# Turning q and k of five more blocks by transposing DMA instead of TensorE, in a sliding-window attention with an MLP behind it

## The chip, the cores and the metric

The kernel runs on one core of one Trainium2 chip. The metric is the device time of one launch in microseconds, as the median of the runs.

## What is computed

Eight batches, eight heads, 576 positions, 64 numbers a head. Attention with an ALiBi bias looks back over at most 128 positions; the heads are laid side by side to rows of 512, which go through a layer norm, an MLP of width 2048 with ReLU, and a residual.

```python
scores = scale * np.matmul(q, k.transpose(0, 1, 3, 2))
rel = pos[:, None] - pos[None, :]
bias = slopes[:, None, None] * (-np.abs(rel).astype(np.float32))[None, :, :]
mask = (rel >= 0) & (rel < window)          # window = 128
scores = np.where(mask, scores + bias[None], -1000000000.0)
attn = softmax(scores)
x = np.matmul(attn, v)                      # then (B, S, H * D)
xn = (x - mu) / np.sqrt(var + 1e-06) * g_ln
out = x + np.maximum(xn @ w_ch1, 0.0) @ w_ch2
```

(The softmax is written out in the reference.) Inputs and outputs are fp32; the kernel loads q, k, v and the weights as fp16, and sums in fp32.

## The kernel before

**Tiles.** The batches go in four pairs p = 0 to 3. A pair has four row blocks i of 128 positions, each for both batches, and a tail i = 4 of 64 positions of each batch together. So a pair has nine blocks of 128 rows, blk = 2i + b for i < 4 and blk = 8 for the tail; n = 9p + blk numbers all 36 (`order`). The third pair is p = 2, its blocks are n = 18 to 26, and its last five are blk 4 to 8, that is i = 2, 3 and 4.

**Loads.** GpSimd issues the loads with a cast to fp16 (`load_qk`, `load_v`), in the order of the list `loads`. The step of block n asks for all loads up to block n + 6 (`load_until`). The raw q and the raw k of a turn each take one of 4 buffers (`raw_pool`), so the load of turn t = 5p + i reuses the buffer of turn t - 4 and waits until that one has been read.

**Turns.** The scores need q and k with the head dimension on partitions. `turn(p, i)` makes that, in one of two ways:

- By TensorE (pairs 0 to 2 before): 64 transposes of 64x64 (32 for a tail) by `transposed()` (L301) into PSUM, with two copies on DVE and two on ACT to SBUF (L333, L334; for a tail one on each, L338). With `in_sc` the PSUM used is that of the score banks, which are marked as `junk`; the next scores in a marked bank are computed whole by `seen()` (L395), otherwise only the parts that the window can see.
- By DMA (pair 3 before): four `dma_start_transpose` of 128x512 on SP (two for a tail, L322), from raw tiles that were loaded in another layout: q in four DMAs of 64 KB and k in two of 128 KB, where the other way has two of 128 KB each; a tail has two and two of 64 KB in both.

`by_dma` tells which way a turn goes.

**Scores and values.** `scores` (L436 the matmuls, L445 the exponential on ACT, L456 the decay mask on DVE), then `values` (L489 on TensorE, L497 and L498 on DVE) give the rows x. `stats` takes mean and variance on DVE (L586, L587) and 1/sqrt on GpSimd (L541, L544); `normal` makes the normed row on DVE (L528) and turns it by a transposing DMA on SP (L536) into xT.

**MLP.** Blocks are gathered in twelve groups: six of two, then six of four; groups 6 to 11 hold blocks 12 to 15, 16 to 19, 20 to 23 and so on. `mlp1` (L730) and `mlp2` (L763) run the two products; from group 6 on `fast_mlp2` (L829) does the second in seven half-size products with sums of `ht` on DVE (L798) and of the results on DVE (L847), over a ring of four PSUM banks. Results are stored by SP (L925; L921 for a tail).

**Order.** TensorE, SP, ACT and DVE run in the order in which the program writes them (`manual_schedule`); GpSimd's order is the scheduler's. `steps` lists the attention work, and `weave_at` puts its steps between units of the MLP (a unit is one `ht` tile of `mlp1`, or one product or part of one in the second half). From block 8 on, an iteration n adds four steps: the values of block n with the scores of block n + 2; masks and stats of n; `turn_at(n + 1)`; `normal(n)`. For a group of four, `mlp1` takes steps at units 0, 2, 5, 7, 8, 10, 13, 15 and `fast_mlp2` at 1, 3, 6, 7, 7, 10, 12, 13. `turn_at` puts a turn by TensorE four iterations ahead of its block and a turn by DMA five:

```python
ahead = [m for m in (n + 3, n + 4) if m < count and order[m][1] % 2 == 0]
return [f for m in ahead if by_dma(order[m][0]) == (m == n + 4) for f in turn_step(m, True)]
```

So the turns of (p, i) = (2, 2), (2, 3) and (2, 4), for blocks 22, 24 and 26, stand in the iterations 18, 20 and 22, and that of (3, 0), for block 27, also in iteration 22.

Of the kernel before, what the change touches and what calls it, by code (L numbers as in the profile page):

```python
# [26 lines left out]
FAST = 6  # L27

NV = 10
BY_DMA_TURN = 3  # L30
AHEAD = 6

FIRST_GROUPS, FIRST = 2, 4
# [26 lines left out]
def kernel(  # L60
# [146 lines left out]

    raw = {}

    def by_dma(p):  # L210
        return p >= BY_DMA_TURN

    def load_qk(src, tag, p, i):

        n = min(P, S - i * P)
        t = raw_pool.tile([P, H, 2, D], FP16, tag=tag, name=tag)
        raw[tag, p, i] = t
        if by_dma(p):
            t = raw[tag, p, i] = t.rearrange("p h r d -> p (h r d)").rearrange(
                "p (b h d) -> p b h d", b=2, h=H  # L220
            )
            for b in range(2):
                rows = src[2 * p + b, :, i * P : i * P + n, :]
                if i == 4:
                    parts = [(t[b * n : (b + 1) * n, 0], rows)]
                elif tag == "k":
                    parts = [(t[:, b], rows)]
                else:
                    rows = rows.rearrange("h (c r) d -> h r c d", r=2)
                    parts = [  # L230
                        (t[r * HALF : (r + 1) * HALF, b], rows[:, r]) for r in range(2)
                    ]
                for dst, part in parts:
                    nc.gpsimd.dma_start(out=dst, in_=part.rearrange("h p d -> p h d"))
            return
        for b in range(2):
            nc.gpsimd.dma_start(  # L237
                out=t[b * n // 2 : (b + 1) * n // 2],
                in_=src[2 * p + b, :, i * P : i * P + n, :].rearrange(
                    "h (c r) d -> c h r d", r=2  # L240
                ),
            )
# [10 lines left out]
    order = [(p, blk) for p in range(NPAIR) for blk in range(NSLOT)]  # L253
# [3 lines left out]
    for n, (p, blk) in enumerate(order):  # L257
        if blk % 2 == 0:
            for src, tag in ((q, "q"), (k, "k")):
                loads.append((load_qk, src, tag, p, blk // 2))  # L260
        loads.append((load_v, p, blk))
        place.append(len(loads))
        loads += weights.get(n, [])
# [14 lines left out]
    def warm(n):  # L278

        if n:  # L280
            ps = ps_mm.tile([P, 4 * P], FP32, tag="mm", name="ps_warm")
        for _ in range(n):
            nc.tensor.matmul(ps, ones[:, 0:P], ones, start=True, stop=True)  # L283
# [7 lines left out]
    def transposed(tag, p, i, ps):  # L291


        st = raw.pop((tag, p, i))
        for hp in range(HP):
            for r in range(2):
                for b, dst in enumerate(ps):
                    rows = slice(b * HALF, (b + 1) * HALF)
                    for j in range(2):
                        cols = slice(j * HALF, (j + 1) * HALF)  # L300
                        nc.tensor.transpose(  # L301
                            dst[cols, r, hp, :],
                            st[rows, 2 * hp + j, r, :],
                            iden[rows, rows],
                        )

    def turn(p, i, in_sc=False, copies=(nc.vector.tensor_copy, nc.scalar.copy)):

        k = keys_tile("k", p, i)
        q = queries(p, i) if i < 4 else keys_tile("q", p, i)
        if by_dma(p):
            for tag, dst in (("q", q), ("k", k)):
                src = raw.pop((tag, p, i))
                for b in range(2 if i < 4 else 1):
                    t = dst[:, b]
                    if tag == "q" and i < 4:  # L320
                        t = turned["q", p, i][:, b].rearrange("p h r c -> p h (r c)")
                    nc.sync.dma_start_transpose(  # L322
                        out=t, in_=src[:, b].rearrange("p h d -> p (h d)")
                    )
            return
        ps = [bank(b if in_sc else None) for b in range(2)]
        if i < 4:
            transposed("q", p, i, [t[:, 0] for t in ps])
            if p == 0 and i == 1:
                warm(3)  # L330
            transposed("k", p, i, [t[:, 1] for t in ps])
            for b, copy in enumerate(copies):
                copy(out=q[:, b], in_=ps[b][:, 0])  # L333
                copy(out=k[:, b].rearrange("p h (c r) -> p r h c", r=2), in_=ps[b][:, 1])  # L334
        else:
            for tag, t, dst, copy in zip("qk", ps, (q, k), copies):
                transposed(tag, p, i, [t[:, 0]])
                copy(out=dst[:, 0].rearrange("p h (c r) -> p r h c", r=2), in_=t[:, 0])  # L338

    def bank(sc=None):  # L340
        if sc is None:
            return ps_mm.tile([P, 2, 2, HP, HALF], FP16, tag="mm", name="ps_tr")
        junk[sc] = True
        return ps_sc[sc][:, 0].bitcast(FP16).rearrange(
            "p (t r h c) -> p t r h c", t=2, r=2, h=HP
        )

    def queries(p, i):
        if by_dma(p):
            t = turned_pool.tile([P, 2, HP, 2, HALF], FP16, tag="q", name="q")  # L350
            turned["q", p, i] = t
            return t
        t = turned_pool.tile([P, 2, 2, HP, HALF], FP16, tag="q", name="q")
        turned["q", p, i] = t.rearrange("p b r h c -> p b h r c")
        return t

    def keys_tile(tag, p, i):
        t = turned_pool.tile([P, 2, HP, P], FP16, tag=tag, name=tag)
        turned[tag, p, i] = t
        return t  # L360

    def turn_first():

        q, k = queries(0, 0), keys_tile("k", 0, 0)
        ps = [bank(b)[:, 0] for b in range(2)]
        transposed("q", 0, 0, ps)
        for b in range(2):
            nc.vector.tensor_copy(out=q[:, b], in_=ps[b])
        ps_row = spread_g()
        warm(2)  # L370
        ps = [bank(b)[:, 0] for b in (0, None)]
        transposed("k", 0, 0, ps)
        for b, copy in enumerate((nc.scalar.copy, nc.vector.tensor_copy)):
            copy(out=k[:, b].rearrange("p h (c r) -> p r h c", r=2), in_=ps[b])
        nc.vector.tensor_copy(out=g_row, in_=ps_row)
# [244 lines left out]
    for g, size in enumerate(GROUPS):  # L620
        n = sum(GROUPS[:g])
# [5 lines left out]
    def turn_step(n, *how):  # L627
        p, blk = order[n]
        return [(turn, p, blk // 2) + how]
# [54 lines left out]
    def turn_at(n):  # L684
        ahead = [m for m in (n + 3, n + 4) if m < count and order[m][1] % 2 == 0]
        return [
            f
            for m in ahead
            if by_dma(order[m][0]) == (m == n + 4)
            for f in turn_step(m, True)  # L690
        ]

    steps.append(turn_at(8))
    for n in range(8, count):
        first_half, second_half = values_steps(n)
        step = first_half + second_half[:1]
        if n + 1 < count and order[n + 1][1] == T:
            step += [(scores_tail, order[n][0])]
        if n + 2 < count:
            step += scores_step(n + 2)  # L700
        steps.append(step)
        steps.append(
            [m for t in (n + 1, n + 2) if t < count for m in masks_of(t)] + [(stats, n)]
        )
        if n + 1 < count:
            steps.append(turn_at(n + 1))
        steps.append([(normal, n)])
# [293 lines left out]
```

## Time and profile before

| | |
|---|---|
| runs of the kernel | median 319.14 us (318.6 to 319.21, three runs) |
| the profiled execution | 318.21 us, span 316.4 us |
| TensorE, matmuls | 305.0 us (96%), granted clock 0.996 of full |
| DVE / ACT / GpSimd | 228.1 us (72%) / 179.3 (57%) / 124.9 (39%) |
| L301, transposes of q and k on TensorE | last at 178.3 us, 864 weight loads |
| L322, transposing DMAs of q and k on SP | 18, from 173.7 us on |
| loads of q and k, GpSimd | L237 60 (pairs 0 to 2), L234 28 (pair 3) |

The chain of waits is followed back from the last instruction: each piece waited for the one before it, so its rows tell what set the end, with start, length, engine, tile, line and count. A timeline has the instructions of one engine in order, and in brackets the idle time before one with what ended it; on SP and GpSimd its times are those in which the engine issues a DMA, and the landing of the data comes later. Seen over 40 slices, TensorE is full from the middle on:

```profile
PE   8989999999898999999999999999999999999994
PEld 2468655857657667555885588548855875685483
DVE  2679787877667698768995889479948995761363
```

By group, TensorE's time goes to the MLP above all:

```profile
L730 PE MATMUL ps_r<-xT,w1g 128*128 128x512 f16 x384 | 85.1, 379 | 0.0
L763 PE MATMUL ps_m<-w,ht 128*128 128x512 f16 x192 | 46.0, 380 | 1.2 <-ACT ht L746 1.2
L829 PE MATMUL ps_r<-w,ht 128*128 128x256 f16 x384 | 44.1, 273 | 0.0
```

The last columns are the busy time of the group, the mean of one in ns, and the idle time of the engine before them with what ended it.

### The profile page before, as it was taken

The numbers are of one execution on the slowest core, as the hardware profiler recorded it, in microseconds if no ns is written. First come the engines' busy times: TensorE is split into PE (matmuls) and PEld (weight loads), VectorE is DVE, ScalarE is ACT, GpSimd is POOL, SyncE is SP. The second block draws the span as 40 slices with busy tenths as digits, with TensorE's granted clock in tenths as the row PEclk, the third lists the DMA queues.
The fourth block names the chain that finished last, engine by engine and source line by source line (L and its number), as shares of the span: only waits on it lengthen the run. The fifth ranks groups of instructions, "written<-read, shape, count | busy, mean of one in ns | idle before, by whom it ended". The sixth has DMA issues, their size and how long they took to land.

```text
span 316.4 us, 9932 instructions
## 1 busy us (share of the span) xinstructions
PE 305.0 (96%) x4195; PEld 205.2 (65%) x4195; DVE 228.1 (72%) x547; ACT 179.3 (57%) x311; POOL 124.9 (39%) x196
## 2 busy tenths in 40 slices
PE   8989999999898999999999999999999999999994
PEld 2468655857657667555885588548855875685483
DVE  2679787877667698768995889479948995761363
ACT  6488765667556658368347832772487247405600
POOL 8923758767155356484345572240001001100000
PEclk9999999999999999999999999999999999999998
DMA  9999999999996999499949994992348044015005
GB/s 111 164 206 199 190 145 184 200 140 149 86 118 79 107 99 157 52 144 68 76 52 158 171 124 53 143 158 52 83 89 132 15 87 86 19 26 125 0 0 136
DMA packets 121183, 34.68 MB, mean 110 GB/s; under 512 B 112049, under 2 KB 116785, under 8 KB 121138
## 3 DMA queue, kind: packets, MB, share of 16 engines
q0 software_dynamic: 89216, 18.36, 71.2%
q1 hardware_dynamic: 31442, 15.15, 25.6%
q8 instruction: 33, 0.54, 0.7%
q10 hardware_dynamic: 480, 0.52, 0.6%
q14 instruction: 12, 0.10, 0.1%
HBM read 36.90 MB, written 9.44 MB: 146 GB/s over the span
## 4 chain that ended last, share of the span: by engine, by line
PE 86%; DVE 6%; ACT 4%; issue 1%; POOL 1%; DVEq 0%; ACTq 0%; POOLq 0%
PE ps_r L730 27%; PE ps_r L829 23%; PE ps_m L763 11%; PE ps_m L730 10%; PE ps_sc L436 5%; PE ps_sc L301 3%; PE ps_r L489 3%; PE ps_pv L489 2%; PE ps_warm L283 2%; ACT probs L445 2%; DVE o L906 1%; DVE x L498 1%; DVE probs L456 1%; DVE o L847 1%; PE ps_tx L581 1%
## 5 line engine op out<-in xcount | busy, mean ns | idle before, releaser
L730 PEld LDWEIGHTS <-w1g 128*128 128x128 f16 x640 | 60.4, 98 | 50.6 <-DVE x L498 1.8
L730 PE MATMUL ps_r<-xT,w1g 128*128 128x512 f16 x384 | 85.1, 379 | 0.0
L445 ACT ACTIVATE probs<-ps_sc 128x1024 f16<-128x1024 f32 x56 | 54.2, 1026 | 51.6 <-PE ps_sc L436 51.5
L746 ACT ACTIVATE ht<-ps_r 128x512 f16<-128x512 f32 x96 | 56.2, 600 | 31.6 <-PE ps_r L730 31.5
L541 POOL TENSOR_TENSOR rstd<-moments,powers 128x1 f32<-128x1 f32 x28 | 6.8, 243 | 102.5 <-DVE moments L587 102.5
L763 PE MATMUL ps_m<-w,ht 128*128 128x512 f16 x192 | 46.0, 380 | 1.2 <-ACT ht L746 1.2
L829 PE MATMUL ps_r<-w,ht 128*128 128x256 f16 x384 | 44.1, 273 | 0.0
L247 POOL DMA_DIRECT2D vx<-in_v_dram x40 | 34.7, 883 | 22.1 <-PE ps_r L489 9.0
L456 DVE TENSOR_TENSOR probs<-probs,m 128x1024 f16<-128x1024 f16 x56 | 37.4, 688 | 7.4 <-ACT probs L445 7.2
L829 PEld LDWEIGHTS <-ht 128*128 128x128 f16 x384 | 37.1, 98 | 4.8
L746 ACT ACTIVATE ht<-ps_m 128x256 f16<-128x256 f32 x91 | 32.9, 391 | 8.5 <-PE ps_m L730 6.2
L730 PE MATMUL ps_m<-xT,w1g 128*128 128x256 f16 x256 | 31.5, 273 | 2.2 <-DVE x L498 0.8
L763 PEld LDWEIGHTS <-ht 128*128 128x128 f16 x192 | 17.1, 98 | 18.8 <-issue 1.3
L237 POOL DMA_DIRECT2D q<-in_q_dram x30 | 20.5, 690 | 17.3 <-PE ps_sc L301 9.3
L586 DVE BATCH_NORM_STATS2 st<-x 128x6 f32<-128x512 f16 x36 | 24.6, 684 | 0.0
L237 POOL DMA_DIRECT2D k<-in_k_dram x30 | 20.2, 687 | 5.8 <-DMA w<-in_moe_w_ch_dram 4.2
L436 PE MATMUL ps_sc<-q,k 64*64 64x128 f16 (+1 forms) x1088 | 20.4, 209 | 1.6 <-ACT probs L445 1.1
L829 PE MATMUL ps_r<-w,hs 128*128 128x256 f16 x192 | 21.9, 273 | 0.0
L489 PEld LDWEIGHTS <-probs 128*128 128x128 f16 x448 | 18.8, 97 | 4.7 <-DVE probs L456 0.3
L829 PEld LDWEIGHTS <-hs 128*128 128x128 f16 x192 | 18.8, 98 | 2.2
L847 DVE TENSOR_TENSOR o<-ps_r,o 128x512 f32<-128x512 f32 (+1 forms) x25 | 16.1, 655 | 5.0 <-PE ps_r L829 4.9
L528 DVE TENSOR_SCALAR xc<-x,moments,rstd 128x512 f16<-128x512 f16 x28 | 12.0, 430 | 10.3 <-POOL rstd L544 10.3
(87 smaller groups left out, 384.3 us busy)
## 6 DMA issues: line engine op xcount, KB each, us to landing
out_dram<-o SPq DMA_DIRECT2D x66, 128.0 KB, 3.1
k<-in_k_dram POOLq DMA_DIRECT2D x32, 128.0 KB, 6.2
vx<-in_v_dram POOLq DMA_DIRECT2D x32, 128.0 KB, 6.7
w<-in_moe_w_ch_dram POOLq DMA_DIRECT2D x8, 512.0 KB, 11.3
q<-in_q_dram POOLq DMA_DIRECT2D x24, 128.0 KB, 4.3
q<-in_q_dram POOLq DMA_DIRECT2D x24, 64.0 KB, 3.8
k<-in_k_dram POOLq DMA_DIRECT2D x8, 64.0 KB, 4.6
vx<-in_v_dram POOLq DMA_DIRECT2D x8, 64.0 KB, 6.4
```

The source lines that it names most:

```text
L237: nc.gpsimd.dma_start(out=t[b * n // 2 : (b + 1) * n // 2], in_=src[2 * p + b, :, i * P : i * P + n, :].rearrange("h (c r) d -> c h r d", ...
L247: nc.gpsimd.dma_start(out=vx[p0 : p0 + n, :, 0:D], in_=v[b, :, t0 : t0 + n, :].rearrange("h p d -> p h d"),)
L436: nc.tensor.matmul(in_halves(ps[cols, j, n, t, :])[:, r, queries], kt[rows, hp, cols], in_halves(qt[rows, b, hp])[:, r, queries], start=Tr ...
L445: nc.scalar.activation(out=dst.rearrange("p (n j) q -> p j n q", j=2), in_=ps.rearrange("p j n t q -> p j n (t q)"), func=AF.Exp, scale=in ...
L456: nc.vector.tensor_tensor(out=dst, in0=dst, in1=mask, op=ALU.mult)
L489: nc.tensor.matmul(ps[:, i, :], pr[:, h, t, :], vext[(p * NSLOT + o) % NV][:, h, :], start=(n == 0), stop=(n == len(terms) - 1),)
L586: nc.vector.bn_stats(out=st, in_=xs[order[n]])
L730: nc.tensor.matmul(ps[:, 0:cols], w[:, kb, fb * P : (fb + 1) * P], xT[:, kb, 0:cols], start=(kb == 0), stop=(kb == NKB - 1),)
L746: nc.scalar.activation(out=ht[:, fb, 0:cols], in_=ps[:, 0:cols], func=AF.Relu)
L763: nc.tensor.matmul(sums[at], ht[:, fb, at * P : (at + 1) * P], w2[:, fb, :], start=(fb == 0), stop=(fb == NFB - 1),)
L829: nc.tensor.matmul(banks[name][pair][:, pair, :], lhs[:, fb, pair * P : (pair + 1) * P], rhs[:, fb, :], start=(first and fb == 0 and (pair ...
L847: nc.vector.tensor_tensor(out=o[:, at, cols], in0=banks[name][at.start][:, at, :], in1=(x if to_x else o)[:, at, cols], op=ALU.add,)
```

## The change

`BY_DMA_TURN` becomes a pair and row block, (2, 2) in place of 3, and `by_dma` takes both. The turns (2, 2), (2, 3) and (2, 4) then go the way of pair 3: loads in the other layout, a contiguous q tile, ten transposing DMAs on SP, and a place one iteration earlier in `turn_at`. The last turn by TensorE is (2, 1).

```diff
-BY_DMA_TURN = 3
+BY_DMA_TURN = (2, 2)
...
-    def by_dma(p):
-        return p >= BY_DMA_TURN
+    def by_dma(p, i):
+        return (p, i) >= BY_DMA_TURN
...
-        if by_dma(p):
+        if by_dma(p, i):
             t = raw[tag, p, i] = t.rearrange("p h r d -> p (h r d)").rearrange(
...
-        if by_dma(p):
+        if by_dma(p, i):
             for tag, dst in (("q", q), ("k", k)):
...
     def queries(p, i):
-        if by_dma(p):
+        if by_dma(p, i):
             t = turned_pool.tile([P, 2, HP, 2, HALF], FP16, tag="q", name="q")
...
-            if by_dma(order[m][0]) == (m == n + 4)
+            if by_dma(order[m][0], order[m][1] // 2) == (m == n + 4)
             for f in turn_step(m, True)
```

## The prediction

> **What bounds the kernel now.** I read the page first: TensorE busy 305.0 of 316.4 us, no other engine above 72%. A mean over stages cannot say what 2 us of TensorE are worth in one of them, so the second view is the chain of waits in the stretch from 140 to 200 us, where the moved work stands:
>
> ```profile
> 143.40 2.70 PE ps_r L730 x12
> 146.09 0.64 PE ps_sc L301 x64
> 146.73 4.42 PE ps_r L730 x20
> ...
> 151.41 0.56 PE ps_sc L436 x16
> ...
> 159.55 0.47 PE ps_sc L436 x16
> 160.02 2.73 PE ps_r L829 x24
> 162.75 0.64 PE ps_sc L301 x64
> 163.40 2.73 PE ps_r L829 x24
> ...
> 167.17 7.01 PE ps_r L730 x32
> ...
> 177.84 0.62 PE ps_sc L301 x32
> 178.46 4.42 PE ps_r L730 x20
> ...
> 191.88 5.35 PE ps_r L829 x48
> ```
>
> Every piece of the chain there is TensorE, and so it goes on to 310 us. The three rows of L301 are the turns that the change takes away: turns (2,2), (2,3) and (2,4), pair and row block counted from 0. The third view, busy time by stretches, agrees: 25.00 of 25 us TensorE in each, at the full clock.
>
> ```profile
> 140.00:165.00 25.00, 25.00 (x405) 17.83 (x403) 20.78 (x45) 15.02 (x22) 9.53 (x18) 1.00 1.00 74
> 165.00:190.00 25.00, 25.00 (x308) 16.07 (x306) 19.12 (x41) 15.55 (x23) 15.92 (x24) 1.00 1.78 149
> ```
>
> The columns behind the stretch are its length, busy PE, PEld, DVE, ACT and POOL, the clock, the DMA share and GB/s. In the table of waits for 140 to 310 us, PE waits for nobody; PEld waits only for its own issue, three times, all before a turn. So in this stage an instruction less on TensorE is time less at the end, unless something else becomes late.
>
> **Removed from TensorE.** A turn costs its transposes and the cut that it makes in the matmuls around it. (2,2): 2.70 + 0.64 + 4.42 = 7.76 us, where the same 32 matmuls uncut take 7.01 (row at 167.17): 0.75. (2,3): 2.73 + 0.64 + 2.73 = 6.10, uncut 48 take 5.35 (row at 191.88): 0.75. (2,4): the piece of 2.70 at 175.13, then 0.62 + 4.42, makes 7.74 against 7.01: 0.73. Sum 2.23; the transposes alone would be 1.90.
>
> A second saving stands in the scores. A turn on TensorE puts fp16 into the score banks and marks them as junk, and the next scores are then computed whole (seen(), L395): 0.56 us at 151.41 against 0.47 at 159.55, where no turn came before. The pieces after the other two turns, at 166.60 and 183.36, are 0.56 too. 3 x 0.09 = 0.27. Together 2.50 us.
>
> The trace has a check on this. Pair 3 is turned by DMA already, and the chain from the values of block 18 to those of block 22 (142.62 to 174.18) holds the same matmuls as from block 27 (213.28, the end of a piece of 7.01 from 206.27) to block 31 (243.13): 31.56 against 29.85, 1.71 for two turns. Block 22 to 25 (174.18 to 197.22) against 31 to 34 (243.13 to 265.35) is 23.04 against 22.22: 0.82. Sum 2.53.
>
> **Removed from ACT and DVE.** The copies out of PSUM: on ACT 2 x (0.59 + 0.74) + 0.73 = 3.4 us, on DVE 2 x (0.42 + 0.72) + 0.70 = 3.0. TensorE waits for neither engine after 140 us, so I count nothing for them.
>
> **Added on SP.** 4 + 4 + 2 transposing DMAs of 128x512. The rows of pair 3 price them:
>
> ```profile
> 167.90 3.25 SPq L925 DMA_DIRECT2D out_dram<-o  x4
> 171.88 1.24 SPq L536 DMA_TRANSPOSE xT<-xc  x1
> 173.73 2.51 SPq L322 DMA_TRANSPOSE q<-q  x2
> 176.42 2.50 SPq L322 DMA_TRANSPOSE k<-k  x2
> 182.35 1.20 SPq L536 DMA_TRANSPOSE xT<-xc  x1
> ```
>
> Four take 5.2 us of SP (173.73 to 178.92), and each lands 4.3 to 5.3 us after its start in this stretch. SP runs in written order, and the turn now goes out one iteration before the one in which TensorE made it, ahead of that iteration's normal(). (2,2) comes behind the stores that end at 136.84: it runs to 142.1 and pushes normal(17)'s xT from 141.71 by 0.4. (2,3) runs from 152.0 to 157.3, in front of normal(19) at 159.3: no push. (2,4) runs from 171.15 to 173.8 and pushes normal(21) from 171.88 by 2, then turn (3,0) from 173.73 to about 175.2, done by 180.4, before 182.35. Who waits for these? xT of blocks 16 to 19 is read by the matmuls at 167.17, of 20 to 23 at 198.19; a push of 0.4 or 2 us lies 15 us or more ahead of that. The one close xT is normal(19), issued 159.3, landed 4.0 later: 3.8 us before its reader, and nothing is pushed before it. The turned tiles land by 146.0, 161.4 and 177.8 and are read by the scores at 159.55, 174.66 and 191.50: 13 us in hand each. Without that cover a late one would be paid in full on TensorE. Cost taken: 0.
>
> One rule speaks against the change: the Trainium skill, "VectorE: DVE Perf Modes", section "The three transpose paths", gives 390 ns for a 128x128 transpose on TensorE and 1309 ns by DMA, and its rules say to use TensorE where PSUM will do as the place of the result. By that, as an estimate, the ten DMAs, forty such squares, would be 52 us, 3.4 times what TensorE would need, and the kernel slower if they lay on its path. The trace does not bear out a loss by it: four squares land in 2.4 to 5.3 us here, and off the chain.
>
> **Added on POOL.** The source now lies in another layout. For (2,2) and (2,3), q comes in four DMAs (2.78 us at 132.70) where it was two (1.45 at 100.35), and k's two take 1.81 where they took 1.38: +1.8 us each. For (2,4), 1.43 + 1.43 for 1.21 + 1.15: +0.5. These loads start at 100.35, 113.58 and 120.66, behind stats() of blocks 11, 13 and 14. The next stats() wait for DVE anyway, 2.39, 2.28 and 1.89 us, which covers +1.8, +1.8 and +0.5. Since the first two leave only 0.6 and 0.5, I keep a bound. What a late stats() costs is seen once, earlier (POOL, DVE and PE in order of time):
>
> ```profile
> 87.26 1.43 POOL L237 DMA_DIRECT2D q<-in_q_dram  x2 [6.92 <-PE ps_sc L301]
> ...
> 90.15 0.41 DVE L528 TENSOR_SCALAR xc<-x,moments,rstd 128x512 f16<-128x512 f16 x1 [1.81 <-POOL rstd L544]
> ...
> 94.86 0.60 PE L730 MATMUL ps_m<-xT,w1g 128*128 128x256 f16 x4 [0.38 <-DMA xT<-xc]
> 96.30 2.24 PE L730 MATMUL ps_m<-xT,w1g 128*128 128x256 f16 x16 [0.84 <-DVE x L498]
> ```
>
> POOL stood 6.92 us at a load whose raw buffer TensorE had not yet freed; the stats() queued behind came 3.4 us late (the moments were there at 85.9, rstd at 90.1 and not 86.7), DVE stood at xc, and TensorE lost 0.38 + 0.84 = 1.2 us. The new POOL time thus costs between 0 and 1.2 us. Nothing here can win: TensorE only waits for POOL or is not affected. I take 0, since the idle time covers it row by row. Its arrival is no issue: these rows are read 30 us and more after they land.
>
> **Moved waits.** The load of turn t reuses the raw buffer of turn t-4, so (3,1), (3,2), (3,3) on POOL now wait for SP's transposes and not TensorE's: free by 146.0, 161.4, 177.8, where TensorE freed them at 146.7, 163.4 and 178.5. None is later than now. Cost 0 if they keep their places among the stats(); the other case is a rival.
>
> **Sum.** 0.75 + 0.75 + 0.73 + 0.27 = 2.50 us less, 0 added. The profiled execution took 318.21 (span 316.4), so it becomes 315.7 with a span of 313.9; the median of the runs is 0.93 above that execution, so the forecast is 319.14 - 2.50 = **316.6**. Its own range, from 1.2 us given back on POOL to 2.53 saved, with 0.6 for the spread of the runs shown: 316.0 to 318.4. What a measurement here can tell from no change is about 0.2%, 0.64 us.
>
> **Rivals.**
> *POOL's order turns against it (slower).* POOL's order is the scheduler's, not written out. If it puts the loads of (3,1), (3,2) and (3,3) ahead of a stats() while their raw buffers are still held by SP's transposes, the stall of 87.26 happens again. At 1.2 us each, three give back 3.6: 319.14 - 2.50 + 3.6 = **320.2**. It decides from the third one on (two are 2.4, just under the saving). For it: it happens in this kernel, and a DVE that stands at xc holds up all evictions. Against it: the buffers come free no later than today, and in this stage DVE itself waits 17.9 us for PE at L497, so lateness is absorbed. Chance 0.10.
>
> *Contention hides the gain (no change).* The DMA share is 1.78 from 165 to 190 us, and ten transposes move 1.3 MB more. If normal(19)'s xT landed 6 us after its start and not 4.0, nothing would follow; TensorE waits only beyond 7.8. For the saving to be lost, 2.5 us beyond that are needed, a landing of about 10; then **319.1**. The longest landing of an xT between 100 and 180 us is 7.1, so 0.08. The Trainium skill, "DMA: Bandwidth & Descriptors", section "Issuing engines are not separate DMA queues", says that transfers of all engines run on the same 16 DMA engines and interleave. The stretch agrees in kind (xT lands in 2.4 to 7.1 us, by what runs beside it), but no row shows it reaching TensorE after 140 us.
>
> *Part is given back,* by one or two stalls of POOL, in the stretch from 100 to 125 us with the longer loads or later at the reused buffers: 317.8 to 319.0, in the middle **318.4**. Chance 0.12.
>
> *The change does not do what it says:* scores read a q of another layout and get slower. The DMA-turned pair has scores of 0.47 like the others, so 0.02, at 319.
>
> **How the numbers follow.** Forecast 0.68, slower 0.10, contention 0.08, part given back 0.12, no effect 0.02. Of the forecast's 0.68 nearly all lies below 318.5, and half of the part given back too: faster 0.73. Contention, the no-effect case and the other half give 0.15 for within 0.2%; slower 0.12, the rival and a tail of contention. The range 315.8 to 319.3 takes in the forecast's own and the cases up to no change, and leaves out the slower one and little below.
>
> **What would show it.** L301 with 160 fewer transposes and nothing later than 132 us; the chain in the stretch with 32 uncut matmuls of 7.0 and 48 of 5.35; all score pieces after 152 us at 0.47 or less; 28 rows of L322 from 137 us on; TensorE without a wait after 140. It would be wrong if the page names a wait of PE for xT or for DVE there, or if POOL shows an idle time ahead of L234 with rstd late behind it.

## The result, and the profile after

The changed kernel takes 333.25 us (332.23 to 334.87, six runs) against 318.70 before: 1.046 times as long, 95% interval 1.0435 to 1.0484. It is 14.5 us slower where 2.5 less were forecast. The profiled execution has a span of 333.1 us.

The page after, in 40 slices of 8.3 us, shows where. TensorE, full here before, has holes from 150 to 200 us, and right behind them its granted clock is down, which before it never was in this stretch:

```profile
PE   8989999999889999995959939999999999999995
...
PEclk9999999999999999999879996999999999999999
```

The table of waits from 95 to 310 us (who waited for whom, us in total, times, longest) has rows that were not there, or small; before, TensorE waited for nobody after 140 us, and DVE waited 5.6 us in all for rstd from there on (after, 25.6 of the 28.4):

```profile
DVE xc L528 <- POOL rstd L544: 28.4, 11, 8.1
POOL q L234 <- DMA q<-q: 25.3, 4, 8.2
...
PEld L829 <- issue: 13.1, 3, 5.5
...
PE ps_r L829 <- DVE x L498: 8.8, 2, 5.3
...
PE ps_r L829 <- DVE o L847: 3.8, 1, 3.8
```

Read from the bottom, TensorE waits for DVE, DVE for GpSimd's rstd, and GpSimd stands at a load that waits for SP's transposes. GpSimd's timeline has it row by row (start, length, line, operation, and in brackets the idle time before and what ended it):

```profile
140.73 0.27 POOL L541 TENSOR_TENSOR rstd<-moments,powers 128x1 f32<-128x1 f32 x1
141.07 0.57 POOL L544 TENSOR_TENSOR rstd<-rstd,powers 128x1 f32<-128x1 f32 x1
149.15 2.78 POOL L234 DMA_DIRECT2D q<-in_q_dram  x4 [7.51 <-DMA q<-q]
153.14 1.78 POOL L234 DMA_DIRECT2D k<-in_k_dram  x2 [1.21 <-issue]
154.93 0.21 POOL L541 TENSOR_TENSOR rstd<-moments,powers 128x1 f32<-128x1 f32 x1
155.22 0.56 POOL L544 TENSOR_TENSOR rstd<-rstd,powers 128x1 f32<-128x1 f32 x1
164.00 2.78 POOL L234 DMA_DIRECT2D q<-in_q_dram  x4 [8.22 <-DMA q<-q]
166.75 1.80 POOL L234 DMA_DIRECT2D k<-in_k_dram  x2
168.53 0.24 POOL L541 TENSOR_TENSOR rstd<-moments,powers 128x1 f32<-128x1 f32 x1
...
184.83 2.79 POOL L234 DMA_DIRECT2D q<-in_q_dram  x4 [3.75 <-DMA q<-q]
...
196.05 1.38 POOL L234 DMA_DIRECT2D q<-in_q_dram  x2 [5.80 <-DMA q<-q]
197.43 0.22 POOL L541 TENSOR_TENSOR rstd<-moments,powers 128x1 f32<-128x1 f32 x1
```

The first pair is the stats of block 17. Then comes the load of turn (3, 1), which now stands ahead of the stats of block 18: the scheduler set GpSimd's order anew. Before, it stood behind them, and the loads of (3, 3) and (3, 4) behind the stats of block 22 (rows of the kernel before: stats of 18, load of (3, 1), stats of 22, loads of (3, 3) and (3, 4)):

```profile
147.11 0.55 POOL L544 TENSOR_TENSOR rstd<-rstd,powers 128x1 f32<-128x1 f32 x1
147.61 2.78 POOL L234 DMA_DIRECT2D q<-in_q_dram  x4
...
178.91 0.56 POOL L544 TENSOR_TENSOR rstd<-rstd,powers 128x1 f32<-128x1 f32 x1
179.43 2.78 POOL L234 DMA_DIRECT2D q<-in_q_dram  x4
...
183.93 1.43 POOL L234 DMA_DIRECT2D q<-in_q_dram  x2
```

The raw buffer of (3, 1) was freed by TensorE before, now by SP's transposes of (2, 2). Those started at 137.44 to 142.3 but landed 8.4 to 9.8 us later, so GpSimd stood until 149.15, issued six DMAs, and came to the stats of block 18 at 154.93, whose moments DVE had ready at 147.2. The load of (3, 2) does the same to block 19, and those of (3, 3) and (3, 4) to block 22.

The second and the third stall each have a part of their own. The transposes of (2, 3), for which the load of (3, 2) waits, landed within 2.5 to 4.5 us, but SP started them only at 157.6 and not near 152: they stand in SP's order behind the xT of block 18, which the first stall made late.

```profile
143.72 13.73 SPq L536 DMA_TRANSPOSE xT<-xc  x2
157.62 2.51 SPq L322 DMA_TRANSPOSE q<-q  x2
```

And the load of (3, 4) reuses the buffer of (3, 0), which went by DMA before the change too. Its wait of 5.80 us is no moved wait: only its place ahead of the stats is new.

On DVE (first fence) and on TensorE (second), the same three places:

```profile
155.82 0.41 DVE L528 TENSOR_SCALAR xc<-x,moments,rstd 128x512 f16<-128x512 f16 x1 [6.03 <-POOL rstd L544]
...
169.45 0.41 DVE L528 TENSOR_SCALAR xc<-x,moments,rstd 128x512 f16<-128x512 f16 x1 [5.80 <-POOL rstd L544]
...
198.90 0.41 DVE L528 TENSOR_SCALAR xc<-x,moments,rstd 128x512 f16<-128x512 f16 x1 [8.08 <-POOL rstd L544]
```

```profile
156.83 3.08 PE L829 MATMUL ps_r<-w,ht 128*128 128x256 f16 x16 [3.44 <-DVE x L498]
...
170.51 5.32 PE L829 MATMUL ps_r<-w,ht 128*128 128x256 f16 x32 [3.80 <-DVE o L847]
...
199.91 3.57 PE L829 MATMUL ps_r<-w,ht 128*128 128x256 f16 x16 [5.33 <-DVE x L498]
```

3.44 + 3.80 + 5.33 = 12.6 us of idle TensorE. The rest is the clock: after each gap the matmuls take longer (16 of them 3.08 us where 16 take 1.92 elsewhere). The next lines are stretches of 2 us behind the first gap, with the granted clock in the third column from the end:

```profile
156.00:158.00 2.00, 1.17 (x9) 0.92 (x9) 1.90 (x7) 0.00 (x0) 0.00 (x0) 0.85 1.33 122
158.00:160.00 2.00, 2.00 (x11) 1.45 (x10) 2.00 (x4) 0.00 (x0) 0.00 (x0) 0.50 0.42 77
160.00:162.00 2.00, 2.00 (x17) 1.63 (x16) 1.97 (x5) 0.00 (x0) 0.00 (x0) 0.80 1.04 76
162.00:164.00 2.00, 2.00 (x27) 1.81 (x25) 1.65 (x3) 0.00 (x0) 0.00 (x0) 1.00 0.47 78
```

TensorE is busy 309.1 us, where 305.0 less the 2.5 of the forecast would be 302.5: 6.6 us more. Behind the three gaps the clock stands at half for some 3.4, 3.2 and 5.3 us of matmuls, which makes 6.0 of them. 12.6 + 6.6 - 2.5 = 16.7, and by 16.7 us the span grew.

### The profile page after: what moved, and what is told of

It reads as the page before. It is cut to its first block, busy times and chain, and to the rows that moved or that the text cites. A ratio compares the mean times of both kernels' runs of the same rounds, so it can differ in the third digit from the quotient of the medians.

```text
span 333.1 us, 9624 instructions
## 1 busy us (share of the span) xinstructions
PE 309.1 (93%) x4035; PEld 206.6 (62%) x4035; DVE 225.7 (68%) x542; ACT 176.2 (53%) x306; POOL 129.3 (39%) x200
## 4 chain that ended last, share of the span: by engine, by line
PE 72%; DMA 8%; DVE 7%; ACT 4%; POOL 4%; issue 3%; SPq 1%; POOLq 0%; ACTq 0%; DVEq 0%
PE ps_r L730 20%; PE ps_r L829 20%; PE ps_m L730 10%; PE ps_m L763 9%; DMA q<-q 4%; PE ps_sc L436 4%; DMA k<-k 3%; ACT probs L445 2%; PE ps_sc L301 2%; PE ps_r L489 2%; PE ps_pv L489 2%; PE ps_warm L283 2%; DMA q<-in_q_dram 1%; POOL q L234 1%; POOL k L234 1%
## 5 line engine op out<-in xcount | busy, mean ns | idle before, releaser
L829 PE MATMUL ps_r<-w,ht 128*128 128x256 f16 x384 | 48.7, 289 | 12.6 <-DVE x L498 8.8
L829 PEld LDWEIGHTS <-ht 128*128 128x128 f16 x384 | 39.3, 103 | 19.8 <-issue 13.1
L234 POOL DMA_DIRECT2D q<-in_q_dram x28 | 19.6, 711 | 25.3 <-DMA q<-q 25.3
L763 PEld LDWEIGHTS <-ht 128*128 128x128 f16 x192 | 17.1, 98 | 18.8 <-issue 1.3
L237 POOL DMA_DIRECT2D q<-in_q_dram x24 | 16.5, 697 | 18.9 <-PE ps_sc L301 9.3
L829 PE MATMUL ps_r<-w,hs 128*128 128x256 f16 x192 | 23.4, 283 | 0.0
L829 PEld LDWEIGHTS <-hs 128*128 128x128 f16 x192 | 19.6, 102 | 3.1
```

The lines of the kernel that those rows point to most:

```text
L237: nc.gpsimd.dma_start(out=t[b * n // 2 : (b + 1) * n // 2], in_=src[2 * p + b, :, i * P : i * P + n, :].rearrange("h (c r) d -> c h r d", ...
L763: nc.tensor.matmul(sums[at], ht[:, fb, at * P : (at + 1) * P], w2[:, fb, :], start=(fb == 0), stop=(fb == NFB - 1),)
L829: nc.tensor.matmul(banks[name][pair][:, pair, :], lhs[:, fb, pair * P : (pair + 1) * P], rhs[:, fb, :], start=(first and fb == 0 and (pair ...
```

## The experiments

Two theories stood at the start. **O**, the order: loads that wait for SP's transposes stand ahead of stats in GpSimd's queue. **L**, lateness: the ten transposes share the DMA engines, so what they and others bring is late, whatever the order. Medians are of three rounds, each beside the kernel before on the same chip.

| run | us | before beside it | ratio, 95% interval |
|---|---|---|---|
| change, written order from group 6 | 315.82 | 318.77 | 0.991 (0.989 to 0.993) |
| before, written order from group 6 | 318.31 | 318.77 | 0.999 (0.997 to 1.001) |
| tail turn alone by DMA | 324.97 | 318.77 | 1.020 (1.018 to 1.023) |
| change, three rstd on DVE | 318.52 | 318.77 | 1.001 (0.998 to 1.003) |
| change, five raw buffers | 327.66 | 318.54 | 1.027 (1.021 to 1.032) |
| two turns by DMA | 330.26 | 318.54 | 1.038 (1.035 to 1.041) |
| five turns, written order from group 4 | 320.09 | 318.54 | 1.005 (1.003 to 1.007) |
| eight turns, written order from group 2 | 318.09 | 318.54 | 0.999 (0.997 to 1.001) |
| change, three loads of v left out | 328.72 | 318.69 | 1.032 (1.027 to 1.036) |
| change, written order from group 2 | 313.26 | 318.69 | 0.983 (0.980 to 0.986) |
| five turns, order from group 2, normal first | 311.56 | 318.69 | 0.978 (0.976 to 0.980) |
| before, written order from group 2 | 315.87 | 318.85 | 0.992 (0.990 to 0.994) |

**GpSimd in written order.** The same edit to the changed kernel and to the one before:

```diff
-            for g in range(6, len(GROUPS)):
+            with tc.manual_schedule(engines={engine.Pool}):
+                for g in range(6, len(GROUPS)):
```

> The changed kernel, with GpSimd too held to the order in which the program writes its work, from group 6 on (its order was the scheduler's). Each load then stands where its step asks for it, two or more iterations after its raw buffer was read. Theory O (GpSimd's order: loads that wait for SP's transposes stand ahead of stats of blocks 18, 19 and 22, DVE stands at xc, TensorE starves): no idle TensorE after 140 us, the clock back at 1.00, and the 2.5 us of the forecast appear: 315.5 to 317.5. Theory L (the ten transposes come late because they share the DMA engines with loads and stores, whatever GpSimd's order): the same transposes move, so the three gaps stay at 3 to 5 us each and the time stays over 328.

> The control to the run above: the kernel before with GpSimd in written order from group 6 on. Both theories: TensorE has no wait after 140 us there to lose, so within 1 us of the kernel before, 317.7 to 319.7. If it is 2 us faster by itself, the gain of the other run is not the change's.

315.82 and 318.31: the gaps are gone and the change is worth 2.49 us between the two, where the forecast had 2.50. Each median is sure to some 0.6 us only, so a match this close is luck. The same ten transposes run here, which speaks against L. But the loads stand elsewhere too (that of (3, 1) goes out at 178.9 us, not at 149.2), so by itself this run leaves L room; the run with rstd on DVE, below, does not. The chain of waits of the changed kernel in this order:

```profile
142.97 0.26 PE ps_r L489 x8
...
143.74 7.01 PE ps_r L730 x32
...
151.48 7.10 PE ps_r L829 x64
...
159.06 0.47 PE ps_sc L436 x16
159.53 5.35 PE ps_r L829 x48
...
196.04 7.01 PE ps_r L730 x32
```

Uncut runs of 32, 64 and 48 matmuls at the lengths that the forecast took, and scores at 0.47. From the values of block 18 to the `mlp1` of blocks 20 to 23 this chain takes 53.07 us (142.97 to 196.04), and in the kernel before 55.57 (142.62 to 198.19): within the traces, too, the change is worth 2.50. The landing of the first four transposes, issued 137.3 to 141.2 us, is short here, least, median and most:

```profile
DMA to landing us min/median/max: 2.4/3.6/4.7
```

**Fewer turns.** `BY_DMA_TURN = (2, 4)`, then `(2, 3)`.

> Only the tail turn (2, 4) goes by DMA, as two transposes; the scheduler then has the loads of (3, 1) and (3, 2) behind the stats again, as before the change, but those of (3, 3) and (3, 4) still ahead of the stats of block 22. Theory O: one stall of three, of the third kind (5.3 us idle, some 2 us more at a lower clock, less the 0.8 us saved): 322 to 327, with DVE's long wait at xc only near 190 to 200 us. Theory L: a fifth of the transposes (2 of 10), so about a fifth of the loss, 3 us: 320.5 to 322, and no single place.

> Turns (2, 3) and (2, 4) by DMA, (2, 2) on TensorE. The scheduler has the load of (3, 2), which waits for the transposes of (2, 3), ahead of the stats of block 19, and those of (3, 3) and (3, 4) ahead of the stats of 22. Theory O: two stalls, so about 318.8 + 6.2 (the tail turn alone cost that) + some 5 for the one at 19 less 0.85: 327 to 331. Theory L (contention in proportion to the transposes moved, 6 of 10): 318.8 + 0.6 x 14.5 = 327.5, which this run can't tell apart; what tells is where TensorE stands idle: O only at two places, behind xc of 19 and of 22.

One stall costs 6.2 us net, two 11.7, three 14.5. Each time TensorE has just that many gaps: one of 5.02 us before 190.55 with the tail alone, two of 4.01 and 5.86 with two turns. The tail alone moves a fifth of the transposes and brings almost half of the loss, more than L allowed. Its row on GpSimd, the load of (3, 3) behind the transposes of (2, 4):

```profile
178.41 2.79 POOL L234 DMA_DIRECT2D q<-in_q_dram  x4 [6.44 <-DMA q<-q]
```

**DVE taken from behind GpSimd's queue.**

```diff
         variance(n)
+        if n in (18, 19, 22):
+            inv_std(n, 1)
+            return
```

> The changed kernel with 1/sqrt of blocks 18, 19 and 22 taken on DVE by the nine small operations that the first blocks use, not on GpSimd, so that DVE no longer stands behind GpSimd's queue there. The scheduler now has the loads of (3, 1) and (3, 2) ahead of the stats of block 20. Theory O: GpSimd still waits 5 us and more for the transposes, but TensorE is not reached by the stalls at 18, 19 and 22; at most a short one at block 20: 316 to 319.5. Theory L: the same transposes beside the same loads, 328 or more.

318.52. The loads still run beside the transposes of (2, 2), which land in 7.1 to 9.2 us, about as late as in the changed kernel, and GpSimd still waits 21.6 us for transposes, in four waits. But TensorE has only one wait after 130 us, 1.3 us. So late transposes alone do not cost the time, and L falls: the way of the loss is GpSimd's queue to DVE to TensorE. It does not reach the 315.8 of the written order; between 145 and 163 us its chain runs over DVE, which has the added operations.

**One buffer more.** Five raw buffers, two output buffers.

> The changed kernel with five raw buffers for each of q and k instead of four (and two output buffers for three, to make room). The scheduler then asks for each load one turn earlier: (3, 2), which waits for the transposes of (2, 2), stands ahead of the stats of block 18, and (3, 3), which waits for those of (2, 3), ahead of those of 19. Theory O: the place in GpSimd's queue decides and not the number of buffers, so two or three gaps of TensorE remain and the time stays between 327 and 335. Rival B (four buffers are too few; one more frees the loads): 316 to 318.

327.66: B falls, in the order that the scheduler makes. It uses the room to ask one turn earlier, and the loads of (3, 2) and (3, 3) wait 6.95 and 6.80 us for transposes, again ahead of stats. TensorE's gaps are 1.65 and 5.33 us, and one of 0.27.

**Contention alone.**

```diff
         vx = vext[(p * NSLOT + blk) % NV]
+        if 25 <= p * NSLOT + blk <= 27:
+            return
```

> The changed kernel without the loads of v for blocks 25, 26 and 27, which GpSimd issues at 137.6 to 140.8 us, just as SP issues the transposes of (2, 2); the rows of those blocks are then computed from old v. The order of the loads of q and k among the stats stays. It prices the part that contention has in the first stall: those transposes landed in 8.4 to 9.8 us, and in 2.4 to 4.7 in the run with the written order, where no loads ran beside them. Theory O with contention as its second factor: they land in 3 to 5 us, GpSimd's wait there falls from 7.5 to 3 us, DVE's wait at xc from 6 to 2, TensorE's first gap from 3.4 us to under 1, the other two stay: 326 to 330. If contention has no part, the first gap stays over 3 us and the time at 332 to 334.

The transposes of (2, 2) land in 4.0 to 7.2 us, not 8.4 to 9.8, which is less of a fall than expected; GpSimd's wait falls from 7.5 to 4.9, DVE's from 6.0 to 0.75, and the first gap is gone, at 4.5 us less. Not all of that is contention: GpSimd also saves the 3.2 us of issuing those loads, and comes to the stats of block 17 some 1.8 us earlier. The second gap (3.5) and the third (4.1) stay. So contention has its part in the size of the first stall, and the order decides whether there is one.

**More turns, and what then bounds.**

> Written order of GpSimd from group 4 on, and all five turns of the third pair by DMA. Theory O: two more turns at 0.85 us each on top of the 2.95 that the written order with three turns gave: 313.3 to 315. If TensorE is not the bound before 135 us, where (2, 0) and (2, 1) stood, the two bring less, 315 to 316; if the order there puts a new wait in, over 316.

> Written order from group 2 on, and from turn (1, 2) on all by DMA, eight turns. Theory O: five turns more than with three, 0.85 each at most where TensorE is the bound, and the old stall of 79 to 87 us gone with GpSimd's order (1.2): 310.5 to 314.5. The other way: in the stage with groups of two an iteration lasts 6 us and the load is asked for less than two iterations ahead of its transposes, so SP stands at the turn and normal() behind it comes late for mlp1: 315 to 320.

Both missed the gain, and the wait is for the late xT that the second named as its other way. In the run with five turns, SP and the chain of waits (two views, two fences):

```profile
127.32 3.52 SPq L322 DMA_TRANSPOSE k<-k  x2
130.93 1.22 SPq L536 DMA_TRANSPOSE xT<-xc  x1
```

```profile
130.93 6.84 DMA xT<-xc
137.78 0.14 issue
137.91 7.16 PE ps_r L730 x22
```

The xT of block 15, the last of group 6, stands behind the transposes of (2, 1) and lands beside loads, 6.8 us after its start; in the kernel before, the two xT there landed in 2.4 and 5.0. TensorE waits 4.9 us for it at `mlp1`. In the run with eight turns it lands after 8.3 us, and TensorE waits 6.2.

**The best version.** Written order from group 2, and with it normal() ahead of the turn:

```diff
-        if n + 1 < count:
-            steps.append(turn_at(n + 1))
         steps.append([(normal, n)])
+        if n + 1 < count:
+            steps.append(turn_at(n + 1))
```

> The changed kernel (turns from (2, 2) on by DMA) with GpSimd in written order from group 2 on instead of from group 6. Theory O: besides the 2.95 us of the run from group 6 on, the old stall of 79 to 87 us goes, in which the same thing happened to a load that waited for TensorE (1.2 us by its rows, up to 2 by TensorE's busy time from 80 to 100 us in the run with eight turns): 313.3 to 315.

> The control to the run from group 2: the kernel before, its turns untouched, with GpSimd in written order from group 2 on. Theory O: the order alone takes the old stall of 79 to 87 us away, 1.2 to 2.5 us: 316.2 to 317.5, so that the three turns by DMA are still worth about 3 us on top. If it reaches 314.5 or less, the turns gave nothing there; if it stays at 318 or more, the old stall cost nothing and the second run's extra gain has another cause.

> Written order from group 2 on, all turns from (2, 0) on by DMA, and in each iteration normal(n) ahead of the turn on SP, so that xT of block 15 is not behind the transposes of (2, 1), which held it up by 5 us in the run from (2, 0). Theory O with SP's order as its twin: 2 x 0.85 below the run from group 2 with three turns: 311.5 to 314. If the transposes are late whatever their place, mlp1 of group 6 still waits for xT and the time is 315 or more.

The order from group 2 on is worth 3.0 us without the change, more than expected; the three turns bring 2.61 on top (315.87 to 313.26). The last run is another 1.70 faster, which is twice 0.85; but it moves normal() as well as turns (2, 0) and (2, 1), so what the two turns alone bring is not shown. TensorE has no wait for xT there any more. The fastest, 311.56, beats the kernel before by 2.2%.

## Why the prediction was wrong

- **Removed from TensorE, 2.50 us: right.** 2.49 and 2.61 between kernels of one order, and 2.50 in the chain. The path was right too: TensorE is the bound there as long as nothing else stalls it.
- **Added on SP: half right.** The four transposes of (2, 2) were put behind the stores, and there they are; "each lands 4.3 to 5.3 us after its start" was a row of (3, 0) at 174 us carried to 137 us, where the loads of (3, 0) and four loads of v had just gone out. They took 8.4 to 9.8. The order of SP was right, but (2, 3) started at 157.6 and not at 152.0, since normal(18) ahead of it was late. The estimate of 52 us for the ten DMAs, 3.4 times what TensorE would need, is not borne out: the forty squares had cost TensorE 1.90 us, and the four of one DMA land in 2.4 to 9.8 us while others are under way. TensorE never waited for the turned tiles at the scores.
- **Added on POOL, up to 1.2: covered,** as the row of idle times said: TensorE is 0.4 us behind the old kernel at 136 us, and was 0.5 behind at 62 us, ahead of all these loads.
- **Moved waits: the step that failed.** "None is later than now. Cost 0 if they keep their places among the stats()". They did not keep them: the scheduler put (3, 1) and (3, 2) ahead of stats 18 and 19, and (3, 3) and (3, 4) ahead of 22. Nor did the buffers come free in time: the first at 149 us for q and 151 for k, not at 146. The term taken as 0 measured 17 us, the 14.5 lost and the 2.5 that the turns should have brought. The prediction's own sign of being wrong, an idle time ahead of L234 with rstd late behind it, is what the trace shows.
- **The rival that came true was undersized.** The prediction had this mechanism as its slower rival, at three stalls of 1.2 us, 320.2, with a chance of 0.10. The three cost those 17 us. The 1.2 was read from one stall in which rstd was 3.4 us late; here it was 7 to 10 late, DVE stood 6 to 8 us, and behind the gaps the clock was halved, which the old gaps of 0.4 and 0.8 never did. Even for the old stall 1.2 may be too little: the order from group 2 on, without it, was worth 3.0, though what else that order brings is not shown apart. The rival also left out (3, 4), whose buffer SP's transposes freed before the change already.
- **The argument against the rival** was that DVE itself waits 17.9 us in the stage and would absorb lateness. It absorbed 2.0 to 2.8 us a time: DVE stood 6.03, 5.80 and 8.08, TensorE 3.44, 3.80 and 5.33.

The Trainium skill, "DMA: Bandwidth & Descriptors", section "Anatomy of one DMA — SWDGE (gpsimd) path", says that DMA engines don't wait on semaphores; the wait happens on the issuing sequencer before dispatch. The trace agrees: the load's wait of 7.51 us is idle time of GpSimd, with the stats behind it.

## What to carry to other kernels

When an edit changes who frees a buffer, look for the instruction that waits for that buffer, and for what stands behind it in its engine's queue: a load that waits on an engine which also computes is a lock on that computation. Where a scheduler sets an engine's order, the order before is no evidence for the order after, so hold the order fixed (here one line) before the change is judged. Price a stall by its own length: a short one seen elsewhere says little of a long one.

## What the runs showed of the hardware

A TensorE gap of 1.65 us left the clock at 1.00; gaps of 3.44 us and more left it at 0.50 for some 3 to 5 us of the matmuls behind them, which made three gaps of 12.6 us cost about 19. The Trainium skill, "TensorE: Matmul & The Clock Gate", section "Why this matters for your kernels", warns of idle gaps over about 3 us between bursts; the trace agrees. And four transposes from SBUF to SBUF, issued from 137 us on in both kernels, took 8.4 to 9.8 us to land behind loads of 64 to 128 KB that GpSimd had issued from 133.1 to 140.8 us; they took 2.4 to 4.7 in the run in written order, where GpSimd issued no load from 124 to 140.1 us. That is one place and two kernels; the run without three of the loads lies between, at 4.0 to 7.2.
